# A pooled attention with a gated convolution FFN: pooling and gate sums shared between VectorE and GpSimd in pieces, the late gates by Sigmoid, and a new order of all the work

## The chip, the cores and the metric

The kernel runs on one core of a Trainium2 chip. The metric is the device time in microseconds, the median of several runs of the same kernel. The core has five engines that work from queues of their own, each in order: TensorE (PE in the profile; its weight loads are PEld), VectorE (DVE), ScalarE (ACT), GpSimd (POOL) and SyncE (SP). SyncE, ScalarE and GpSimd also issue DMAs from their queues. Engines wait for each other through semaphores.

## The reference

Eight sequences of 576 positions, eight heads of 64. Keys and values are averaged over eight positions, so attention is over 72 pooled keys; its result feeds an FFN whose hidden layer is gated by the sigmoid of a three-tap convolution along the sequence.

```python
def _attn_ref(q, k, v):
    B, H, S, D = q.shape                      # 8, 8, 576, 64
    k_p = k.reshape(B, H, S // 8, 8, D).mean(axis=3)
    v_p = v.reshape(B, H, S // 8, 8, D).mean(axis=3)
    scores = np.matmul(q, k_p.transpose(0, 1, 3, 2)) / np.sqrt(D)
    scores = scores - np.max(scores, axis=-1, keepdims=True)
    attn = np.exp(scores)
    attn = attn / (np.sum(attn, axis=-1, keepdims=True) + 1e-09)
    return np.matmul(attn, v_p)

def _moe_ref(x, w_in, conv_w, w_out):         # x: 8 x 576 x 512, w_in: 512 x 1024
    h = np.maximum(x @ w_in, 0.0)
    hp = pad(h, one row of zeros at both ends)
    conv_out = sum(conv_w[j] * hp[:, j:j + S] for j in range(3))
    gate = 1.0 / (1.0 + np.exp(-conv_out))
    return h * gate @ w_out
```

## The kernel before

**Order.** The kernel first describes its work as a graph of operations (`Graph.add`): each has the engines that may do it, what it must follow, and the buffers that it uses. A long list, `Graph.ORDER`, then says in which order the operations are emitted and, by the last bit of each number, on which of two engines; `Graph.PLACES` says which buffer of a ring, or which PSUM bank, each one gets, and `Graph.FORMS` which of two matmul shapes. Nothing is planned while the program is built: the lists are the outcome of a planner that ran earlier. Since every engine takes its queue in order, an operation that waits holds back all that stands behind it on its engine.

**Tiles.** The sequences go in four pairs, called groups g = 0 to 3. A group has nine attention tiles of 128 rows (group 0 has ten), 37 in all. Each tile holds all eight heads.

**Preparing.** All inputs are loaded by DMAs that GpSimd issues (`load_q`, `load_v`, `load_pair`, lines 272 to 308), which also convert to bfloat16. For v, VectorE adds halves three times (L471: 1280, 640 and 320 elements a partition) and spreads the sums under a mask of heads (`prep_v`, L475). For k of sequences 2 to 7 it does the same on a pair at once (`pool_pair`, L424: 2304, 1152, 576 elements), and TensorE turns the result (L430, L453); k of sequences 0 and 1 is pooled by a matmul with a pooling matrix. q is turned by TensorE (L501, L505) and copied out of PSUM by VectorE or ScalarE (L519), or by a DMA in group 3.

**Attention, one tile.** Scores on TensorE (L567, L580); the maximum on VectorE (L593); the shift by it on VectorE (L605) or, in group 0, on TensorE (L613); Exp on ScalarE (L631); a transpose by TensorE (L642) and a copy (L656), or by a DMA from SyncE's queue in groups 2 and 3; the product with v on TensorE (L667); a reciprocal and a division on VectorE (L680, L682); and a second transpose to xT, by TensorE (L699) and a copy (L707), or by DMA.

**FFN, one sequence.** For each of eight blocks of 128 hidden channels: eight matmuls of 288 columns (L712) and a ReLU on ScalarE (L721) into hT. The gate is made for four blocks (a half, `f4`) at a time, in one of two ways:
- *by TensorE* (`ffn_conv`, L874): 64x64 matmuls with diagonal weights. Because of the way in which these are packed, the gate of every second block comes out with its two halves of partitions swapped. Tanh (L899) writes even blocks to gT and odd ones to a tile tg; then VectorE adds one to the even ones (L910, 1152 elements) and adds one and swaps for the odd ones (L912, two instructions of 64 partitions). Sequences 4 to 7 have copies at both ends of hT, made on GpSimd (`ffn_wrap`, L796, L797), so that each tap is one run of columns.
- *by taps* (six halves of sequences 4 to 7, `TAPS`): ScalarE multiplies by the middle tap (L847), VectorE adds the two others (L849), Tanh (L854), and VectorE adds one (L860, 2304 elements).

Sigmoid is thus made as (1 + tanh(x/2)) / 2, with the half in the ReLU's scale. VectorE multiplies the gate by h (L920, L861), and TensorE multiplies by w_out for each of 36 row tiles (`ffn_out`, L928, eight matmuls of 512 columns); the result is copied (L939) and stored (L951), mostly from SyncE's queue.

There are two buffers each for hT, gT and xT, one for k, three for v, four for q.

Of the kernel before, what the change touches and what calls it, by code (L numbers as in the profile page):

```python
# [16 lines left out]

# [6 lines left out]
class Op:  # L24
    def __init__(self, engines, key, emit, uses, mode, land, count):
        self.engines, self.key, self.emit, self.mode, self.land, self.count = engines, key, emit, mode, land, count
        self.uses, self.next, self.left = list(uses), [], 0
        self.forms, self.like, self.dmas = None, None, 1
        self.ready, self.start, self.end, self.engine = 0.0, None, None, None
        for t in self.uses:  # L30
            t.users.append(self)


class Graph:

    SPARES = 150
    ATT = 90.28  # L40
    SPREAD = -122.92
    PREP_K = 135.88
    KPOOL = -99.86
    KTURN = 15.09
    PREP_Q = 1123.0
    PREP_V = 2242.18
    GATE = 390.96
    CONV = 199.25
    QCONV = -794.87
    OUT = 412.5  # L50
    LAST = 1107.48
    FIRST = 803.11
    V0 = -1430.11
    DW = -368.65
    X_DMA = 4
    APART = (0,)
    SIXTEEN = ()
    Q_DMA = (3,)
    WRAP = (4, 5, 6, 7)
    TAPS = ((4, 1), (5, 0), (5, 1), (6, 0), (6, 1), (7, 0))  # L60
    ACC = 2
    WRAPS = 2
    CROSS = ()
    BY_TILE = ()
    V_POOL = ()
    K_POOL = ()
    SHIFT_PE = ((0, 0), (0, 1), (0, 2), (0, 3), (0, 4), (0, 5), (0, 6), (0, 7), (0, 8), (0, 9))
    TURN_DMA = 2
    BANKS = 8
    ORDER = (  # L70
# [107 lines left out]
def kernel(  # L178
# [17 lines left out]
    C = 9  # L196
# [1196 lines left out]
```

## Time and profile before

| | |
|---|---|
| median of 3 runs | 220.81 us (220.59 to 220.98) |
| span of the profiled execution, from its first to its last instruction | 224.8 us |
| mean granted TensorE clock in it | 0.979 |
| last copy of a result ends | 220.3 us after the span's start |

The profiled execution has no other time of its own than its span; the span is longer than the timed runs, since the profiler was on. Rows of the profile name the line of the kernel, the engine and operation, the tiles written and read, the count, the busy time and the mean of one; behind the bar stands the engine's idle time just before them and what ended most of it.

### The profile page before, as it was taken

The numbers are of one execution on the slowest core, as the hardware profiler recorded it, in microseconds if no ns is written. First come the engines' busy times: TensorE is split into PE (matmuls) and PEld (weight loads), VectorE is DVE, ScalarE is ACT, GpSimd is POOL, SyncE is SP. The second block draws the span as 40 slices with busy tenths as digits, with TensorE's granted clock in tenths as the row PEclk, the third lists the DMA queues.
The fourth block names the chain that finished last, engine by engine and source line by source line (L and its number), as shares of the span: only waits on it lengthen the run. The fifth ranks groups of instructions, "written<-read, shape, count | busy, mean of one in ns | idle before, by whom it ended". The sixth has DMA issues, their size and how long they took to land.

```text
span 224.8 us, 6558 instructions
## 1 busy us (share of the span) xinstructions
PE 205.1 (91%) x2722; PEld 137.9 (61%) x2722; DVE 195.4 (87%) x337; ACT 160.9 (72%) x271; POOL 45.1 (20%) x81
## 2 busy tenths in 40 slices
PE   5897999979999999959999949989999999999991
PEld 1465778755788877636677735656656665654450
DVE  7889876999999999957999948999999999999641
ACT  2155768898999958844697935688889999997210
POOL 7943321131230120000000121001031230540000
PEclk9999999999999999988999988999999999999997
DMA  5999999999999999947664553168566617423495
GB/s 81 137 191 207 207 206 208 207 207 206 207 208 206 155 187 172 207 39 163 121 106 92 119 118 76 32 92 165 117 145 140 137 23 166 95 48 71 96 247 194
DMA packets 48833, 32.61 MB, mean 145 GB/s; under 512 B 28300, under 2 KB 44324, under 8 KB 48804
## 3 DMA queue, kind: packets, MB, share of 16 engines
q0 software_dynamic: 16288, 16.26, 44.8%
q1 hardware_dynamic: 31796, 14.96, 33.3%
q10 hardware_dynamic: 720, 0.98, 1.5%
q8 instruction: 21, 0.34, 0.6%
q14 instruction: 8, 0.07, 0.1%
HBM read 32.52 MB, written 9.44 MB: 187 GB/s over the span
## 4 chain that ended last, share of the span: by engine, by line
PE 44%; DVE 30%; DMA 8%; issue 7%; ACT 6%; POOL 3%; DVEq 0%; POOLq 0%
PE psum L928 21%; PE psum L712 14%; DVE negm L593 6%; DMA qp<-in_q_dram 6%; DVE x L682 5%; DVE sd L605 5%; PE psum L874 4%; DVE tg L849 2%; DVE gT L912 2%; PE psum L667 2%; DMA eT<-e 2%; DVE v L471 2%; DVE r L680 2%; DVE gT L920 2%; ACT e L631 1%
## 5 line engine op out<-in xcount | busy, mean ns | idle before, releaser
L712 PE MATMUL psum<-xT,w_in_sb 128*128 128x288 bf16 x512 | 74.4, 289 | 0.8 <-ACT tg L899 0.5
L928 PE MATMUL psum<-w_out_sb,gT 128*128 128x512 bf16 (+1 forms) x296 | 70.3, 378 | 0.5 <-DVE gT L920 0.5
L712 PEld LDWEIGHTS <-w_in_sb 128*128 128x128 bf16 x512 | 48.4, 99 | 17.6 <-issue 1.6
L721 ACT ACTIVATE hT<-psum 128x576 bf16<-128x576 f32 x64 | 40.1, 652 | 14.9 <-PE psum L712 14.3
L928 PEld LDWEIGHTS <-gT 128*128 128x128 bf16 x296 | 27.7, 98 | 27.0 <-issue 1.2
L849 DVE SCALAR_TENSOR_TENSOR tg<-hT,convw,tg 128x576 f32<-128x576 bf16 x48 | 37.3, 818 | 0.4
L593 DVE TENSOR_REDUCE negm<-psum 128x8 f32<-128x576 f32 (+2 forms) x37 | 27.4, 750 | 4.4 <-PE psum L567 3.9
L796 POOL COPY hT<-hT 128x126 bf16<-128x126 bf16 x16 | 9.1, 567 | 101.4 <-ACT hT L721 90.9
L682 DVE TENSOR_TENSOR x<-psum,r 128x512 bf16<-128x512 f32 (+1 forms) x37 | 25.6, 691 | 1.3
L667 PE MATMUL psum<-vm,eT 128*128 128x130 bf16 (+5 forms) x240 | 20.0, 227 | 4.1 <-DMA eT<-e 2.9
L874 PE MATMUL psum<-hT,dw 64*64 64x288 bf16 (+2 forms) x608 | 19.2, 261 | 2.6 <-issue 2.3
L667 PEld LDWEIGHTS <-eT 128*128 128x128 bf16 (+1 forms) x240 | 16.0, 103 | 9.1 <-DMA eT<-e 3.8
L605 DVE TENSOR_TENSOR sd<-psum,negm 128x576 f32<-128x576 f32 x27 | 20.1, 752 | 1.0 <-ACT e L631 0.5
L631 ACT ACTIVATE e<-sd 128x576 bf16<-128x576 f32 x27 | 18.6, 689 | 1.8 <-DVE sd L605 1.6
L874 PEld LDWEIGHTS <-dw 64*64 64x64 bf16 x608 | 14.8, 107 | 7.6 <-issue 6.7
L847 ACT ACTIVATE tg<-hT,convw 128x576 f32<-128x576 bf16 x24 | 18.0, 773 | 1.0 <-DVE gT L912 0.9
L899 ACT ACTIVATE tg<-psum 128x576 bf16<-128x576 f32 x20 | 13.0, 653 | 7.2 <-PE psum L874 7.2
L939 ACT COPY osb<-psum 128x512 f32<-128x512 f32 x25 | 14.5, 586 | 4.0 <-PE psum L928 3.9
L854 ACT ACTIVATE gT<-tg 128x576 bf16<-128x576 f32 x24 | 16.2, 685 | 0.8 <-DVE tg L849 0.3
L471 DVE TENSOR_TENSOR v<-v 128x1280 bf16<-128x1280 bf16 (+2 forms) x24 | 13.0, 540 | 2.1 <-DMA v<-in_v_dram 1.9
L899 ACT ACTIVATE gT<-psum 128x576 bf16<-128x576 f32 x20 | 12.9, 649 | 2.0 <-PE psum L874 2.0
L920 DVE TENSOR_TENSOR gT<-gT,hT 128x2304 bf16<-128x2304 bf16 x10 | 13.5, 1349 | 0.0
(82 smaller groups left out, 236.2 us busy)
## 6 DMA issues: line engine op xcount, KB each, us to landing
out_dram<-osb SPq DMA_DIRECT2D x54, 128.0 KB, 2.4
v<-in_v_dram POOLq DMA_DIRECT2D x8, 512.0 KB, 15.2
qp<-in_q_dram POOLq DMA_DIRECT2D x7, 576.0 KB, 16.9
kk<-in_k_dram POOLq DMA_DIRECT2D x3, 1152.0 KB, 17.6
out_dram<-qp SPq DMA_DIRECT2D x10, 128.0 KB, 2.9
w_in_sb<-in_moe_w_in_dram POOLq DMA_DIRECT2D x2, 512.0 KB, 17.3
w_out_sb<-in_moe_w_out_dram POOLq DMA_DIRECT2D x1, 1024.0 KB, 24.3
out_dram<-qp ACTq DMA_DIRECT2D x6, 128.0 KB, 2.7
```

What stands on the lines that cost most here:

```text
L593: nc.vector.tensor_reduce(out=a["m"][0:rows], in_=a["s"][0:rows, :, 0:2 * KW].rearrange("p a (h s) -> p a h s", s=Sp), axis=AX.X, op=OP.ma ...
L605: nc.vector.tensor_tensor(out=a["d"][0:rows], in0=a["s"][0:rows, :, 0:2 * KW].rearrange("p a (h s) -> p a h s", s=Sp), in1=a["m"][0:rows]. ...
L631: nc.scalar.activation(out=dst, in_=src, func=ACT.Exp, scale=1.0 / (POOL * 8.0),)
L667: nc.tensor.matmul(out=a["o"][lo:hi, h // 4, (h % 4) * (D + 1):(h % 4 + x1 - x0) * (D + 1)], lhsT=a["eT"][:, j, lo:hi], rhs=buf("vm", b)[: ...
L682: nc.vector.tensor_tensor(out=a["x"][0:rows].rearrange("p (a h d) -> p a h d", a=2, d=D), in0=ov[:, :, :, 0:D], in1=r[0:rows].unsqueeze(3) ...
L712: nc.tensor.matmul(out=banks(ps)[:, j, 0:SC], lhsT=w_in_block(dc, fb), rhs=buf("xT", g)[:, dc, i * S + j * SC:i * S + (j + 1) * SC], start ...
L721: nc.scalar.activation(out=h_of(b)[:, fb].rearrange("p (a s) -> p a s", a=2), in_=banks(ps)[:, :, 0:SC], func=ACT.Relu, scale=0.5,)
L847: nc.scalar.activation(out=acc, in_=h, func=ACT.Identity, scale=w)
L849: nc.vector.scalar_tensor_tensor(out=acc, in0=h, scalar=w, in1=acc, op0=OP.mult, op1=OP.add)
L874: nc.tensor.matmul(out=banks(pss[r ^ c])[c * D:(c + 1) * D, j, lo:hi], lhsT=dw[r * D:(r + 1) * D, tap * n_fb + fb, :], rhs=hT[r * D:(r + 1 ...
L899: nc.scalar.activation(out=t.rearrange("p (a s) -> p a s", a=2), in_=banks(ps)[:, :, 0:SC], func=ACT.Tanh, scale=0.5,)
L928: nc.tensor.matmul(out=bank(ps)[0:rows, columns], lhsT=buf("gT", g)[:, fb, t * P:t * P + rows], rhs=w_out_sb[:, fb, columns], start=(fb == 0),
```

## The change

1. **Pieces on two engines.** The three additions of k and v and the spread of v are cut (k: three, two and one pieces; v: two, one, one and two), and each piece may be done by VectorE or GpSimd, as the order says. The three raisings of a gate (adding one, and the swap) become operations of their own that may go to either engine too.
2. **Sigmoid for late gates.** For sequences 5, 6 and 7 ScalarE computes Sigmoid instead of Tanh. The adding of one falls away there; only the swap of odd blocks stays, as a copy. ReLU has the scale 1 there instead of 0.5. Sigmoid and Exp are in different function tables, so all Sigmoids follow all Exps, and one table load stands between them.
3. **Choices by tile.** Shift, both transposes and the form of the gate are chosen tile by tile in a table, `CHOICE`. ReLU may go to VectorE, clearing to GpSimd, stores of all groups to ScalarE's queue.
4. **No end copies for the gates made by TensorE**; 64 matmuls for a pair of blocks everywhere, where sequences 4 and 7 had 48.
5. **A new order**: new lists, made by a planner in which VectorE gives way to GpSimd, and which was run under three sets of durations. The matmuls that filled TensorE's early waits (L384, 22) are no longer in the list.

How many instructions each engine gets, in the two programs:

| | before | after |
|---|---|---|
| VectorE: raisings of gates | 36 | 11 |
| VectorE: pooling and spread of k and v | 41 | 37 |
| GpSimd: raisings of gates | 0 | 20 |
| GpSimd: pooling and spread of k and v | 0 | 29 |
| GpSimd: end copies | 32 | 24 |
| VectorE, ScalarE: copies of turned Exps | 2, 17 | 9, 10 |
| VectorE, ScalarE: ReLU | 0, 64 | 6, 58 |
| ScalarE: table loads | 1 | 2 |
| ScalarE's queue: stores | 9 | 26 |
| TensorE: fills | 22 | 0 |

```diff
-    def pool_pair(g, step):
-        t, half = buf("kk", g), POOL * D >> step + 1
-        engine = nc.gpsimd if g in Graph.K_POOL else nc.vector
+    def pool_pair(g, step, cs, engine):
+        t, half = buf("kk", g)[:, cs], POOL * D >> step + 1
         engine.tensor_tensor(out=t[:, :, 0:half], in0=t[:, :, 0:half], in1=t[:, :, half:2 * half], op=OP.add)
...
+    def raise_gate(engine, b, fb, out, in_):
+        if graph.chosen("sigma", b, fb // 4):
+            engine.tensor_copy(out=out, in_=in_)
+        elif engine is nc.gpsimd:
+            engine.tensor_scalar(out=out, in0=in_, scalar1=1.0, scalar2=1.0, op0=OP.mult, op1=OP.add)
+        else:
+            engine.tensor_scalar(out=out, in0=in_, scalar1=1.0, scalar2=None, op0=OP.add)
...
+    def gate_func(b, fb):
+        return ACT.Sigmoid if graph.chosen("sigma", b, fb // 4) else ACT.Tanh
...
-    def ffn_gate(b, f4):
+    def ffn_gate(b, f4, part, engine):
...
-        nc.vector.tensor_scalar(out=gate[:, 0], in0=gate[:, 0], scalar1=1.0, scalar2=None, op0=OP.add)
-        for r in range(2):
-            nc.vector.tensor_scalar(
-                out=gate[r * D:(r + 1) * D, 1], in0=tg[(1 - r) * D:(2 - r) * D], scalar1=1.0, scalar2=None, op0=OP.add
-            )
+        if part == 2:
+            raise_gate(engine, b, 4 * f4, gate[:, 0], gate[:, 0])
+            return
+        raise_gate(engine, b, 4 * f4, gate[part * D:(part + 1) * D, 1], tg[(1 - part) * D:(2 - part) * D])
...
+    def fast(instructions, n, two=True):
+        return {"DVE": instructions * (0.065 + n * (0.00052 if two else 0.00026)),
+                "POOL": instructions * (0.1 + n * (0.00198 if two else 0.00091))}
...
+        for step, cuts in ((0, (0, 3, 6, 9)), (1, (0, 5, 9)), (2, (0, 9))):
+                o = add(fast(1, (hi - lo) * (POOL * D >> step + 1)), None, after=before or [loads["kk", g]], uses=[kk[g]])
+                then(o, lambda o, step=step, cs=cs: pool_pair(g, step, cs, hand(o)))
...
+        for step, cuts in enumerate(((0, 3, 5), (0, 5), (0, 5), (0, 3, 5))):
+                o = add(fast(1, (hi - lo) * (POOL * D >> step + 1 if step < 3 else 3 * D)), None,
...
+    for o in sigmas:
+        for e in exps:
+            graph.follow(e, o)
```

Here `fast` holds the durations that the planner worked with for the divisible operations, `hand` gives the engine that the order chose, and `sigmas` and `exps` are all Sigmoid and all Exp operations.

More of the change, by code (lines that the diff above doesn't have):

```diff
@@ L24, with __init__ @@
 class Op:
-    def __init__(self, engines, key, emit, uses, mode, land, count):
-        self.engines, self.key, self.emit, self.mode, self.land, self.count = engines, key, emit, mode, land, count
+    def __init__(self, engines, emit, uses, mode, land, count):
+        self.engines, self.emit, self.mode, self.land, self.count = engines, emit, mode, land, count
         self.uses, self.next, self.left = list(uses), [], 0
-        self.forms, self.like, self.dmas = None, None, 1
-        self.ready, self.start, self.end, self.engine = 0.0, None, None, None
+        self.forms, self.dmas, self.engine = None, 1, None
         for t in self.uses:
@@ L985, with add_load @@
-    seq = [START]
-    def nudge(kind, b):
-        return 0.0
-    def soon():
-        seq[0] += 0.01
-        return seq[0]
-    loads = {}
-    kk, kp, qp, qTt = {}, {}, {}, {}
-    kb = B and H * S * D * 4
-    def add_load(kind, b, key, share=1.0, **part):
+    n_outs = {b: [t for t in range(9) if (t < 4) == (i == 0)] for b, (g, i) in where.items()}
+    kb = H * S * D * 4
+    loads, kp, qp, qTt = {}, {}, {}, {}
+    kk0 = token("kk", 0)
+    kk = {0: kk0}
+    def add_load(kind, b, share=1.0, **part):
@@ L1032 @@
-    p0 = add({"POOL": 1.6}, first("pm"), build_pool_matrix, after=[c1])
-    add_load("q", 0, first("q0"), 4 / 9, cs=slice(0, 4))
-    c0 = add({"POOL": 0.55}, first("ident"), lambda: make_identity(nc, ident))
-    z0 = add({"DVE": 0.3}, soon(), lambda: clear(buffers["kT"][0]))
-    idf = add({"ACT": 0.3}, soon(), lambda: nc.scalar.copy(out=ident_f, in_=ident), after=[c0])
-    cwtok = token("ps")
-    cwp = add({"PE": 0.1}, soon(), lambda: turn_conv_weights(cwtok), after=[idf, cwl], uses=[cwtok], count=2)
@@ L1047 @@
-    hmw = add(dve(1.15), soon(), widen_mask, after=[hm])
-    dw0 = add({"DVE": 0.3}, soon(), lambda: build_conv_matrices(0, cwtok), after=[cwp], uses=[cwtok])
-    dwo = [add({"DVE": 1.0}, START + Graph.DW + n, lambda n=n: build_conv_matrices(n), after=[dw0]) for n in (1, 2)]
-    win = [add({"POOL": 0.74}, first("w%d" % j), lambda j=j: load_w_in(j), land=(LATE, 2 * P * d_ff * 4, RATE)) for j in range(2)]
-    wout = add({"POOL": 0.9}, first("out"), load_w_out, land=(LATE, d_ff * d_model * 4, RATE))
@@ L1053, in add_load_pair @@
+    def add_load_pair(g):
         kk[g] = token("kk", g)
[L1054 to L1057 removed]
+        loads["kk", g] = add({"POOL": 1.03}, lambda: load_pair(g), uses=[kk[g]], land=(1.3, 2 * kb, 1))
+    for b in range(1, B):
         if b == 1:
[L1059 to L1063 removed]
@@ L1211, in add_att @@
-        xdone[g, t] = o
-    hdone, gdone, htok, gtok = {}, {}, {}, {}
+        for by_dma in graph.options("out", (0, 1) if g else (0,), g, t):
+            if by_dma:
+                outs.append(add({"SP": 1.29}, lambda: att_out(g, t), after=[o], uses=[x, xtok[g]], land=(1.4, 0, 1)))
+            else:
+                sm2 = token("ps")
+                p = add({"PE": 0.223}, lambda sm2=sm2: att_turn_out(g, t, sm2), after=[o], uses=[sm2, x],
+                        mode=FULL if rows == P else (64, 128), count=8)
+                p = add(either(0.42, 0.59), None, after=[p], uses=[sm2, xtok[g]])
+                outs.append(then(p, lambda p: att_copy_out(g, t, copier(p))))
@@ L1308, in add_out @@
-    def add_out(b, w):
-        w += nudge("o", b)
+        relu = {}
+        for fb in range(n_fb):
+            big, o = token("ps", n=2), None
+            for j in range(2):
+                o = add({"PE": 0.49}, lambda fb=fb, j=j, big=big: ffn_in(b, fb, j, big),
+                        after=half_of(b, j) + [win[fb // 4], o], uses=[big, xtok[g]], mode=FULL, count=8)
+            o = add({"ACT": 0.565, "DVE": 0.665}, None, after=[o], uses=[big, htok[b]])
+            relu[fb] = [then(o, lambda o, fb=fb, big=big: ffn_relu(b, fb, big, o))]
@@ L1344 @@
[L1344 to L1359 removed]
+            o = add(either(0.69, 0.585), None, after=[o] + free, uses=[osb, sm])
@@ new lines, in add_out, with queue @@
+            then(o, lambda o, t=t, sm=sm: ffn_copy(g, t, sm, copier(o)))
+            o = add({"SP": 1.3, "ACT": 1.16}, None, after=[o], uses=[osb], land=(2.4, 0, 1))
+            then(o, lambda o, t=t: ffn_store(g, t, queue(o)))
+    def queue(o):
+        return nc.scalar if o.engine == "ACT" else nc.sync
+    for b in range(B):
+        if b < 2:
+            add_prep_k(b)
+        elif b % 2 == 0:
+            add_pair(b // 2)
+        add_prep_q(b)
+        add_prep_v(b)
+    for b in range(B):
+        for t in n_tiles[b]:
+            add_att(where[b][0], t)
@@ L1361 @@
+    for b in range(B):
+        add_ffn(b)
+        add_out(b)
+    for o in sigmas:
+        for e in exps:
+            graph.follow(e, o)
     with tc.manual_schedule():
```

687 lines of the change are left out of this document (294 added, 393 removed), and 121 rows, old and new, of tables (ORDER, PLACES).

## Prediction

> **What bounds the kernel now.** I read the page's span and busy rows first, then the windows, then the end of the chain of waits. The windows' columns are the stretch, its length, and each engine's busy time with its instruction count; then the granted clock, the DMA share and GB/s.
>
> ```profile
> span 224.8 us, 6558 instructions
> PE 205.1 (91%) x2722; PEld 137.9 (61%) x2722; DVE 195.4 (87%) x337; ACT 160.9 (72%) x271; POOL 45.1 (20%) x81
> PE 44%; DVE 30%; DMA 8%; issue 7%; ACT 6%; POOL 3%; DVEq 0%; POOLq 0%
> 0.00:40.00 40.00, 33.98 (x572) 24.07 (x575) 32.35 (x78) 21.61 (x36) 19.20 (x37) 1.00 1.11 177
> 40.00:166.60 126.60, 118.05 (x1799) 83.02 (x1788) 115.72 (x196) 98.81 (x168) 15.45 (x28) 0.97 0.84 145
> 0.00:166.60 166.60, 152.03 (x2359) 107.08 (x2360) 148.06 (x273) 120.42 (x203) 34.66 (x65) 0.98 0.91 153
> 163.10:219.90 56.80, 56.60 (x384) 32.45 (x380) 50.42 (x70) 43.55 (x74) 12.24 (x20) 1.00 0.51 120
> 162.82 0.30 PE L567 MATMUL psum<-kT,qT 64*64 64x72 bf16 x16
> 180.01 1.47 PE psum L712 x12
> 179.15 0.86 PE psum L928 x4
> 219.85 0.42 DVE qp L939
> ```
>
> The kernel has two long stages. From 163.1 us, when the last attention tile's scores leave TensorE (the L567 row), to 219.9 us, TensorE is busy 56.6 of 56.8 us, and at its peak: the chain gives 1.47 us for 12 matmuls of L712 (0.1225 each) and 0.86 for 4 of L928 (0.216 each). After those scores the built program has 128 of L712, 180 of L928, 24 of L667 and 48 of L874; 128 x 0.1225 + 180 x 0.216 is 54.6 us, which leaves 2.2 for the other 72, about 0.03 each. This stage is as long as TensorE's work in it.
>
> Ahead of that, from 40 to 166.6 us (the last maximum), VectorE is busy 115.7 of 126.6 us. TensorE's 118.1 is no better evidence: a small matmul shows its latency as busy time (that stage has 1799 in 118 us, the last one 384 in 57), and the chain of waits gives VectorE 30% of the span, most of it in this stage. So the time of the last scores is VectorE's, and the rest of the span is TensorE's. The span is 4.0 us above the median of the timed runs, 220.81; I sum against the span and multiply by 220.81 / 224.8 = 0.982.
>
> **The change on VectorE.** I counted both built programs' VectorE instructions ahead of the last maximum, and priced them by these rows (pieces of other sizes by a line through the three sizes of L471 and L424: some 0.15 us + 0.52 ns an element).
>
> ```profile
> L849 DVE SCALAR_TENSOR_TENSOR tg<-hT,convw,tg 128x576 f32<-128x576 bf16 x48 | 37.3, 818 | 0.4
> L920 DVE TENSOR_TENSOR gT<-gT,hT 128x2304 bf16<-128x2304 bf16 x10 | 13.5, 1349 | 0.0
> L912 DVE TENSOR_SCALAR gT<-tg 64x1152 bf16<-64x1152 bf16 x20 | 9.1, 455 | 0.3
> L910 DVE TENSOR_SCALAR gT<-gT 128x1152 bf16<-128x1152 bf16 x10 | 5.3, 530 | 0.0
> L860 DVE TENSOR_SCALAR gT<-gT 128x2304 bf16<-128x2304 bf16 x6 | 4.8, 800 | 0.1
> L471 DVE TENSOR_TENSOR v<-v 128x1280 bf16<-128x1280 bf16 x8 | 6.5, 818 | 1.9 <-DMA v<-in_v_dram 1.9
> L471 DVE TENSOR_TENSOR v<-v 128x640 bf16<-128x640 bf16 x8 | 3.9, 485 | 0.1
> L471 DVE TENSOR_TENSOR v<-v 128x320 bf16<-128x320 bf16 x8 | 2.5, 318 | 0.1
> L475 DVE TENSOR_TENSOR vm<-v,mask_wide 128x960 bf16<-128x960 bf16 x8 | 5.2, 651 | 0.1
> L424 DVE TENSOR_TENSOR kk<-kk 128x2304 bf16<-128x2304 bf16 x3 | 4.0, 1347 | 0.0
> L682 DVE TENSOR_TENSOR x<-psum,r 128x512 bf16<-128x512 f32 x35 | 24.2, 692 | 1.2
> L519 DVE COPY qT<-psum 128x1152 bf16<-128x1152 bf16 x4 | 3.0, 751 | 0.7 <-PE psum L501 0.7
> L656 DVE COPY eT<-psum 128x640 bf16<-128x640 bf16 x1 | 0.5, 480 | 0.0
> L939 DVE COPY osb<-psum 128x512 f32<-128x512 f32 x2 | 1.4, 683 | 0.0
> ```
>
> - Gate sums (L912 18 to 5, L910 9 to 2, L860 1 to none): 13 x 0.455 + 7 x 0.530 + 0.8 = 10.4 us off.
> - Pooling of v and its spread (L471 and L475, 18.2 us in 32 instructions) becomes 25 smaller ones, 11.0 us: 7.2 off. Pooling of k (7.7 us in nine) becomes twelve, 6.2: 1.5 off. The clearing of e goes to GpSimd: 0.5 off.
> - Copies that come to VectorE: seven of eT (3.5 us, less one short one), three of qT (2.0), two of osb (1.4), one ReLU (about 0.7); two of kT leave (0.6): 7.0 us on.
> - Order: 7 fewer of L849, 2 fewer products L920, 2 fewer divisions and one shift stand ahead of the last maximum: 5.7 + 2.7 + 1.8 + 0.7 = 11 us later, not saved.
>
> That is 23.6 us less. By the same rows the program before sums to 160.6 us there, while the windows give 148.06 busy: neighbours overlap, so a summed microsecond is 0.92 elapsed, and 23.6 become 21.7. Over the whole program the counts fall by 12.9 us summed, 11.9 elapsed; the rest is order.
>
> **On TensorE.** The later work comes back behind the last scores: the changed program has 168 of L712 there, 200 of L928, 36 of L667 and 96 of L874. That is 40 x 0.1225 + 20 x 0.216 + 60 x 0.03 = 11.0 us more, 67.8 in all. Ahead of them it loses these 11.0 and the fills' 7.8 (row below) from its 152.0 busy: 133, which fits into the 145 to 150 us that VectorE will need. Behind them VectorE holds about 57 us and ScalarE about 50, DMA issues included; both stay under 67.8, so I put nothing there for the Sigmoid's table load (1.28 us, below), the six ReLUs on VectorE or nine stores moved to ScalarE's queue at 1.2 us a pair. If that cover went, these would cost about 1.3, 4 and 11 us.
>
> ```profile
> L1036 ACT ACT_TABLE_LOAD x1 | 1.3, 1283 | 0.8 <-PEq L1377 0.8
> 212.23 1.21 ACTq L951 DMA_DIRECT2D out_dram<-qp  x2
> L384 PE MATMUL psum<-gT 128*128 128x448 bf16 x22 | 7.8, 463 | 2.8 <-DVE gT L1027 2.5 <-ACT eT L656 0.2
> ```
>
> Sigmoid takes as many ScalarE instructions as Tanh, and saves the raising of five four-block groups (L860, 0.8 each): inside the VectorE counts. Two half-sequences give up their wrapping copies on GpSimd (8 of 32), and their convolution takes 64 matmuls a pair of blocks instead of 48, counted in L874. All Sigmoids wait for the last Exp; 17 ReLUs remain behind it against 15 before, so the wait moves no bound. The 22 filling matmuls (L384, 7.8 us) go; they stood where TensorE waited for loads. Without them the first real matmuls may run slower, and the second half of k now queues on GpSimd behind the pooling matrix: I put 0.6 us for both, from 0 to 2.
>
> **What GpSimd costs VectorE.** GpSimd gets 20 raisings of 1152 elements and 29 additions and products of 15,744 elements in all. Rows that show what two such engines do to each other (min/median/max in ns):
>
> ```profile
> 4.20 1.66 POOL L316 TENSOR_SCALAR_AFFINE_SELECT gT<-gT 64x648 bf16<-64x648 bf16 x2
> 4.28 0.78 DVE L372 TENSOR_TENSOR ident<-ident 128x64 bf16<-128x64 bf16 x1
> L376 DVE TENSOR_TENSOR dw<-ident,convw x2: 948/1257/1566, 5.1 to 30.1; 128x768 bf16<-128x768 bf16 x2
> L910 DVE TENSOR_SCALAR gT<-gT x10: 441/452/911, 42.5 to 207.8; 128x1152 bf16<-128x1152 bf16 x10
> L796 POOL COPY hT<-hT x16: 294/530/1452, 126.9 to 201.7; 128x126 bf16<-128x126 bf16 x16
> L849 DVE SCALAR_TENSOR_TENSOR tg<-hT,convw,tg x48: 800/814/892, 130.4 to 204.2; 128x576 f32<-128x576 bf16 x48
> ```
>
> VectorE's addition of 64 elements at 4.28 us took 0.78, until GpSimd's first selection was over; its next one took 1.57 against 0.95 without a neighbour. GpSimd's 0.29 us copies took up to 1.45 beside VectorE. So the one that starts second waits. The Trainium skill says it as a rule, in "SBUF — State Buffer", section "Who interferes with whom": VectorE instructions with two SBUF inputs, or in a mode with two ports, and GpSimd instructions that read SBUF lock each other out for a whole instruction, and those that read PSUM never wait. By that rule the trace agrees.
>
> In the stage from 40 us to the last maximum 48 of the changed VectorE instructions are of that kind (12 of k, 10 of v, 3 spreads, 7 raisings, 8 products, 8 taps); some 118 read PSUM, among them the maxima and divisions. Unit price from below: beside the late copies L849 never lost more than 0.892 - 0.800 = 0.09 us; 48 x 0.1 = 4.8. From above: the three hits above cost 0.5 to 0.7 us. GpSimd's own rate is not shown for these forms; L316 gives 1.2 ns an element with one input, so 28 us for the raisings and 19 to 38 for the two-input pieces, 47 to 66 us, about half of a stage of 100: half of 48 at 0.6 is 14.4. I take 4.8, because the copies too run beside a busy VectorE, in an order, not at random; below zero nothing can come of it.
>
> The Trainium skill's "GPSIMD Engine Reference", section "Performance versus the Vector engine", gives about 2.6 cycles an element for two inputs at 1.2 GHz: an estimate of 34 us for the 15,744 elements. That lies inside the bounds above and moves no term.
>
> **Sum.** 224.8 - 21.7 + 11.0 + 4.8 + 0.6 = 219.5 us of span, times 0.982: 215.6 us.
>
> **Rivals.**
> 1. *The lock costs more than was saved* (slower). Break-even is where lock and start cost 10.7 us, or 0.21 us for each of the 48. For it: a piece of 1 us or more is longer than the 0.29 us copies. At 14.4 the time is 225.0; at 20 it is 230.5. Against it: 118 neighbours that read PSUM, beside which a piece can run. Chance 0.18. The Trainium skill's rule, applied to an order that does not avoid it, is this case.
> 2. *GpSimd's queue becomes late* (slower). It executes in order, and each wait for ScalarE's gates, a landed load or the port holds every load and piece behind it.
>
> ```profile
> POOL v L290 <- DVE vm L475: 13.9, 2, 7.2
> v<-in_v_dram POOLq DMA_DIRECT2D x8, 512.0 KB, 15.2
> ```
>
>    A v load takes 15.2 us to land, and such loads already waited 13.9 us for free buffers. With 47 to 66 us of pieces and some 25 of issues, GpSimd has 72 to 91 of about 100 us. If one chain of k or v comes one load late, TensorE loses up to 15 us: 230; one half late, 223. Chance 0.10.
> 3. *A gain beyond the forecast*: the order hides the lock and the start entirely, 224.8 - 21.7 + 11.0 = 214.1, which is 210.3; and if a third of VectorE's 10.9 us of idle between 40 and 166.6 us goes too, 206.7. Chance 0.15.
> 4. *Nothing left over*: order and lock cancel the relief; 220 to 221.5. Chance 0.10, of which 0.04 within the bound, 0.04 faster, 0.02 slower.
>
> The forecast, a lock of 2 to 8 us, gives 212.8 to 218.7; chance 0.47. Between these, the sum says 0.66 for faster by over 0.2% (0.2%, 0.44 us, is about what a measurement of this kernel can tell), 0.04 for no difference, 0.30 for slower. The range that leaves out no more than 2 in 10 goes from 209.5 to 226.
>
> **What would show it.** Right: VectorE's busy time about 182 (195.4 - 11.9 and some waiting), the last scores (line L552 of the changed kernel) near 147 us, then a TensorE stage of 68 us without gaps, raisings on GpSimd of 1 to 1.5 us. Wrong: products and taps on VectorE well above 1.36 and 0.82 us (rival 1); idle VectorE or TensorE that GpSimd's pieces end (rival 2); gaps behind the last scores that a Sigmoid ends.

## The result and the profile after

The changed kernel takes 230.64 us (median of 4 runs, 229.07 to 231.72) against 220.89 for the kernel before, measured beside it: ratio 1.0448, 95% interval 1.0388 to 1.0507. It is 4.5% slower. The forecast was 215.6 us, with a range that ended at 226. The medians here and below are over all runs, while the ratios leave out runs that lie over 1.5% above the fastest of the same kernel.

The page of the changed kernel: span, busy rows, and the chain that ended last, by engine.

```profile
span 228.8 us, 6686 instructions
PE 200.4 (88%) x2752; PEld 139.5 (61%) x2768; DVE 192.7 (84%) x318; ACT 150.7 (66%) x253; POOL 105.0 (46%) x128
PE 54%; DVE 20%; issue 8%; DMA 8%; ACT 4%; POOL 3%; ACTq 0%; DVEq 0%; POOLq 0%
```

VectorE was forecast at some 182 us busy and has 192.7. This execution took 230.63 us, its span plus 1.83, and the three others took 1.82 to 1.87 us more than their spans. So the note ahead of the prediction, that the span is longer than the runs because the profiler was on, is wrong: a span of 224.8 us belongs to a run of some 226.6 us, and the profiled execution of before was a long one. Another execution of the unchanged kernel before (e1_before, 222.17 us) is the better partner. These are its window up to the last maximum, the line of the scores, whose last start is 158.5 us, and in the timeline the last copy of a result.

```profile
0.00:162.10 162.10, 149.30 (x2342) 106.85 (x2359) 147.43 (x273) 120.13 (x203) 35.47 (x65) 1.00 0.93 157
```

```profile
L567 PE MATMUL psum<-kT,qT x312: 189/195/217, 12.5 to 158.5; 64*64 64x72 bf16 x156
```

```profile
215.43 0.42 DVE L939 COPY qp<-psum 128x256 f32<-128x256 f32 x1 [0.46 <-PE psum L928]
```

The changed kernel has these rows for the same, with the window behind the last scores:

```profile
0.00:157.30 157.30, 134.83 (x2272) 100.60 (x2281) 134.54 (x239) 100.60 (x172) 90.52 (x106) 0.96 0.95 155
155.90:224.10 68.20, 66.98 (x504) 40.01 (x500) 59.15 (x81) 51.25 (x84) 14.83 (x23) 1.00 0.53 118
```

```profile
L552 PE MATMUL psum<-kT,qT x296: 190/195/265, 14.4 to 155.8; 64*64 64x72 bf16 x148
```

```profile
224.12 0.42 DVE L891 COPY qp<-psum 128x256 f32<-128x256 f32 x1 [0.96 <-PE psum L880]
```

Behind the last scores TensorE is busy 66.98 of 68.20 us; 67.8 was forecast. Before, that stage lasted from 158.5 to about 215.4, 57 us. Ahead of them the change was to save 16.3 us (21.7 less 4.8 and 0.6) and saved 2.7 (158.5 to 155.8). The whole miss lies there. VectorE's busy time up to the last maximum did fall by 12.9 us (147.43 to 134.54), but its idle time rose by 8.1 (14.7 to 22.8). By the forecast 21.7 - 4.8 = 16.9 us were to come off, and all of it was to shorten the front.

The groups that answer the questions on GpSimd (line, engine, operation, count, busy time, mean in ns):

```profile
L785 POOL TENSOR_SCALAR gT<-tg 64x1152 bf16<-64x1152 bf16 x11 | 15.1, 1375 | 4.7 <-ACT tg L853 4.0
L872 DVE TENSOR_TENSOR gT<-gT,hT 128x2304 bf16<-128x2304 bf16 x16 | 26.4, 1656 | 0.0
L410 DVE TENSOR_TENSOR kk<-kk 128x768 bf16<-128x768 bf16 x6 | 4.8, 824 | 0.0
L410 DVE TENSOR_TENSOR kk<-kk 128x640 bf16<-128x640 bf16 x3 | 2.4, 802 | 0.0
L410 DVE TENSOR_TENSOR kk<-kk 128x512 bf16<-128x512 bf16 x1 | 1.4, 1402 | 0.0
L787 DVE TENSOR_SCALAR gT<-tg 64x1152 bf16<-64x1152 bf16 x7 | 4.0, 574 | 0.2
L815 DVE SCALAR_TENSOR_TENSOR tg<-hT,convw,tg 128x576 f32<-128x576 bf16 x48 | 37.6, 815 | 0.6
```

The products take 1.656 us in the mean against 1.349 before: 16 x 0.307 is 4.9 us. The mean hides two kinds: five of them take 2.26 to 2.44 us, the other eleven 1.35 to 1.36. VectorE's additions of v, which nothing disturbed, take 0.550, 0.484 and 0.417 us for 768, 640 and 512 elements in this trace; by these those of k lost 1.6, 1.0 and 1.0, and the gate sums 7 x 0.119 = 0.8. That is 9.3 us of locked VectorE time. All but one product's 0.95 us of it, some 8.4 us, stands ahead of the last maximum, where 4.8 was taken and 14.4 was the upper bound. The taps (L815) lost nothing.

Three stretches show where TensorE stands. First the kernel before (e1_before), then the changed one:

```profile
40.00:60.00 20.00, 17.32 (x323) 12.04 (x316) 19.08 (x32) 18.30 (x32) 4.07 (x5) 1.00 1.24 207
70.00:80.00 10.00, 9.73 (x173) 8.17 (x172) 9.74 (x21) 8.90 (x17) 1.01 (x1) 1.00 1.00 159
130.00:140.00 10.00, 9.46 (x94) 5.97 (x96) 8.96 (x16) 6.23 (x11) 1.92 (x5) 1.00 0.48 100
```

```profile
40.00:60.00 20.00, 15.82 (x402) 12.61 (x395) 15.64 (x27) 13.82 (x24) 12.68 (x16) 0.83 1.09 183
70.00:80.00 10.00, 7.71 (x133) 6.00 (x132) 8.70 (x13) 6.03 (x12) 9.67 (x8) 0.83 1.07 133
130.00:140.00 10.00, 8.20 (x117) 5.86 (x115) 9.41 (x13) 6.42 (x12) 5.57 (x6) 0.90 0.50 81
```

In these 40 us TensorE of the changed kernel is busy 4.8 us less, and what it does it does at a granted clock of 0.83, 0.83 and 0.90 where before had 1.00. Each holds one pause of 1.8 to 2.3 us and half clock in it or behind it.

### The profile page after: what moved, and what is told of

Its sections match the earlier page's. It is cut to its first block, busy times and chain, and to the rows that moved or that the text cites. A ratio compares the mean times of both kernels' runs of the same rounds, so it can differ in the third digit from the quotient of the medians.

```text
span 228.8 us, 6686 instructions
## 1 busy us (share of the span) xinstructions
PE 200.4 (88%) x2752; PEld 139.5 (61%) x2768; DVE 192.7 (84%) x318; ACT 150.7 (66%) x253; POOL 105.0 (46%) x128
## 4 chain that ended last, share of the span: by engine, by line
PE 54%; DVE 20%; issue 8%; DMA 8%; ACT 4%; POOL 3%; ACTq 0%; DVEq 0%; POOLq 0%
PE psum L880 21%; PE psum L697 18%; DVE x L667 5%; PE psum L838 4%; DMA out_dram<-osb 4%; DMA v<-in_v_dram 4%; PE psum L652 3%; DVE kk L410 2%; DVE gT L872 2%; DVE negm L578 2%; DVE sd L590 2%; PE psum L684 2%; PE psum L627 2%; DVE r L665 1%; DVE gT L787 1%
## 5 line engine op out<-in xcount | busy, mean ns | idle before, releaser
L880 PE MATMUL psum<-w_out_sb,gT 128*128 128x512 bf16 (+1 forms) x280 | 65.9, 373 | 1.2 <-issue 0.5
L713 ACT ACTIVATE hT<-psum 128x576 bf16<-128x576 f32 x58 | 37.3, 650 | 12.6 <-PE psum L697 12.2
L815 DVE SCALAR_TENSOR_TENSOR tg<-hT,convw,tg 128x576 f32<-128x576 bf16 x48 | 37.6, 815 | 0.6
L578 DVE TENSOR_REDUCE negm<-psum 128x8 f32<-128x576 f32 (+3 forms) x37 | 27.4, 754 | 9.5 <-PE psum L565 4.5
L872 DVE TENSOR_TENSOR gT<-gT,hT 128x2304 bf16<-128x2304 bf16 x16 | 26.4, 1656 | 0.0
L590 DVE TENSOR_TENSOR sd<-psum,negm 128x576 f32<-128x576 f32 (+1 forms) x26 | 19.6, 755 | 1.8 <-ACT e L616 0.5
L616 ACT ACTIVATE e<-sd 128x576 bf16<-128x576 f32 (+1 forms) x26 | 17.6, 681 | 4.1 <-DVE sd L590 1.5
L785 POOL TENSOR_SCALAR gT<-gT 128x1152 bf16<-128x1152 bf16 x9 | 11.5, 1280 | 18.9 <-ACT gT L820 15.7
L456 POOL TENSOR_TENSOR v<-v 128x320 bf16<-128x320 bf16 (+3 forms) x14 | 18.2, 1304 | 2.1 <-DVE v L456 1.5
L820 ACT ACTIVATE gT<-tg 128x576 bf16<-128x576 f32 x24 | 16.3, 682 | 3.3 <-DVE tg L815 3.3
L891 ACT COPY osb<-psum 128x512 f32<-128x512 f32 x20 | 11.6, 580 | 8.8 <-PE psum L880 7.3
L785 POOL TENSOR_SCALAR gT<-tg 64x1152 bf16<-64x1152 bf16 x11 | 15.1, 1375 | 4.7 <-ACT tg L853 4.0
## 6 DMA issues: line engine op xcount, KB each, us to landing
qp<-in_q_dram POOLq DMA_DIRECT2D x7, 576.0 KB, 14.7
kk<-in_k_dram POOLq DMA_DIRECT2D x3, 1152.0 KB, 16.3
```

The costliest lines, as they stand in the source:

```text
L456: engine.tensor_tensor(out=vt[:, :, 0:half], in0=vt[:, :, 0:half], in1=vt[:, :, half:2 * half], op=OP.add)
L578: nc.vector.tensor_reduce(out=a["m"][0:rows], in_=a["s"][0:rows, :, 0:2 * KW].rearrange("p a (h s) -> p a h s", s=Sp), axis=AX.X, op=OP.ma ...
L590: nc.vector.tensor_tensor(out=a["d"][0:rows], in0=a["s"][0:rows, :, 0:2 * KW].rearrange("p a (h s) -> p a h s", s=Sp), in1=a["m"][0:rows]. ...
L713: nc.scalar.activation(out=out, in_=banks(ps)[:, :, 0:SC], func=ACT.Relu, scale=scale)
L785: engine.tensor_scalar(out=out, in0=in_, scalar1=1.0, scalar2=1.0, op0=OP.mult, op1=OP.add)
L815: nc.vector.scalar_tensor_tensor(out=acc, in0=h, scalar=w, in1=acc, op0=OP.mult, op1=OP.add)
```

## The experiments

All times are medians; the ratio is to the kernel before, measured beside each.

**The bases: e1_before and e10_after**, both kernels unchanged.

> The kernel before, unchanged, profiled once more. Theory A (the profiled execution of before was a long one): the span is about 219.0, since the changed kernel's runs take 1.83 us more than their span, and 220.8 less 1.83 is 219.0; the stalls near 96 us and 129 us are then shorter. Theory B (before's profiled execution was a typical one and its span stands 4 us above its runs): the span is 224 to 225 again, with both stalls. Time 220.8 in both.

> The changed kernel, unchanged, once more, as the base of these runs: 229 to 233, with TensorE's pause of about 2.3 us in the middle of the transposes L490 near 50 us, and the half clock behind it, if that pause belongs to the program; without it, if it was chance.

e1_before: 221.84 us, ratio 0.9964 (0.9907 to 1.0021), with a span of 220.4. Theory A holds in kind: the profiled execution of before was 4.4 us longer than this one. e10_after: 230.71, ratio 1.043 (1.033 to 1.053), and the pause near 50 us is there again, 2.37 us at the same transposes. It belongs to the program.

**Is VectorE the bound of the front? e11_before_relief, e15_before_conv1, e20_both.** The kernel before, with work left out on VectorE, on TensorE, and on both.

```diff
 # e11: no pooling additions (pool_pair, prep_v steps 0 to 2)
+        return
 # e15: conv_todo, both forms
-for tap in (1, 0, 2)
+for tap in (1,)
 # e20: both edits
```

> The kernel before, with VectorE's 33 additions that pool k and v left out (20.6 us of VectorE, all ahead of the last maximum; GpSimd, ScalarE and the order as before; k and v are not pooled). If VectorE alone sets the time of the last maximum, as the prediction had it, 221 less 0.92 x 20.6 = 19: 201 to 205. If round trips between the engines stand right behind it, the relief is paid only in part: 207 to 217, VectorE's idle time ahead of the last maximum rising from 14.7 us to 20 or more.

> The kernel before with only the middle tap of the convolution in its matmul form (the outer taps are left out there): some 420 small TensorE matmuls less, most of them ahead of the last scores, VectorE and the rest as before. Theory D (TensorE is the bound of the front): 0.0215 us each, 8 to 10 us off, 211 to 214. The prediction's view (VectorE sets the time of the last scores): 219 to 221, since only what lies behind the last scores counts.

> The kernel before without VectorE's 33 pooling additions and without the outer taps of the matmul form of the convolution (k and v are not pooled, the convolution is not complete). If VectorE and TensorE stand level in the front, the two reliefs pay together what neither paid alone: 207 to 213. If loads or round trips hold both: 216 to 219, no more than the 3 us of the taps alone.

Measured: 220.93 (ratio 1.0018, 0.9969 to 1.0067); 218.36 (0.9883, 0.9845 to 0.992); 214.87 (0.9695, 0.9619 to 0.9771). Taking 20.6 us of work from VectorE ahead of the last maximum moved nothing. This is the run that refutes the prediction's first step. Its window up to the last maximum stands first, then the chains by engine of e1_before, e11, e15 and e20, each over the whole span:

```profile
0.00:161.00 161.00, 150.23 (x2361) 106.98 (x2362) 131.42 (x240) 120.02 (x203) 35.47 (x65) 1.00 0.95 158
```

```profile
PE 38%; DVE 36%; DMA 10%; issue 8%; ACT 5%; POOL 0%; DVEq 0%
```

```profile
PE 52%; DVE 21%; DMA 8%; issue 6%; ACT 6%; POOL 3%; SPq 0%; DVEq 0%; POOLq 0%
```

```profile
DVE 51%; PE 22%; issue 12%; DMA 5%; ACT 5%; POOL 3%; DVEq 0%; ACTq 0%; POOLq 0%
```

```profile
DVE 34%; PE 27%; DMA 16%; ACT 9%; issue 8%; POOL 4%; DVEq 0%; ACTq 0%; POOLq 0%
```

With VectorE relieved its busy time falls to 131.4 of 161 us, and the chain goes from VectorE (36 to 21%) to TensorE (38 to 52%); with TensorE relieved, it goes to VectorE (51%). Neither relief alone pays more than 3 us (0 and 2.6 by the ratios); together they pay 6.4 (6.7 by the ratio), more than the sum of both and still short of the 8 us at the near end of what was expected, and then the chain holds 16% of landing loads. So the front of before has VectorE and TensorE level within a few us, with the loads and round trips not far behind. What I expected of e15 (8 to 10 us) was too much for the same reason.

**What the pieces on GpSimd bring in the new order: e2_all_dve, e3_gate_dve, e14_k_dve.** The changed kernel, its pieces back on VectorE: all, the gate sums, the pooling of k.

```diff
             o.engine = list(o.engines)[0 if n < 0 else n % 2]
+            if o.kind in Graph.BACK:     # ("k", "v", "gate"), ("gate",), ("k",)
+                o.engine = "DVE"
```

> The changed kernel in its own order, with every divided piece that GpSimd does (29 of the pooling of k and v and its spread, 20 gate sums, the clearings) on VectorE, some 22 us more work there by VectorE's own rows. Theory A (what GpSimd takes off VectorE comes back nearly whole, as locked VectorE instructions, some 10 us, and as waits for late pieces): 227 to 234, products L872 back at 1.35 us. Theory B (the pieces do save VectorE's time, and the new order and the start lose it again): 240 to 250. Theory C (late pieces of GpSimd are most of the loss): under 224.

> The changed kernel in its own order, with only the 20 gate sums of GpSimd back on VectorE (20 x 0.46 to 0.53, 10 us more there). Theory A: the sums beside the products make much of the lock, so 226 to 233, and L872 near 1.4 us. Theory B: 236 to 241. Theory C: under 225 if the late pieces are gate sums, about 240 if they are k and v.

> The changed kernel with only GpSimd's pieces of k's pooling back on VectorE (some 5 to 6 us more there). Theory D, if the pause at 75 us (2.19 us, ended by a k addition) comes from late or locked pieces: it falls under 1 us, and the time is 227 to 230 in spite of the added work. If VectorE is the bound there: 233 to 237.

Measured: 243.89 (ratio 1.0992, 1.0899 to 1.1085), 233.96 (1.0561, 1.0464 to 1.0659) and 234.83 (1.0628, 1.0543 to 1.0714). In the order that was made for them the pieces are worth 13 us in all; theories A and C fall for e2, and B was right. e3 came out between A and B. So GpSimd as such is not where the time goes: the kernel is slower in spite of it. e14's time is that of its last case, VectorE as the bound: the pause at 75 us did fall, from 2.19 to 1.27 us, but others of about 2 us came at 79 and 126.

**The pieces left out: e5_left_out, e18_half_left.** GpSimd's in-place additions of k and v and its nine in-place gate sums return without an instruction; e18 has the transposes of e13 (below) as well.

```diff
 # pool_pair, prep_v (steps 0 to 2), ffn_gate part 2, raise_gate on one view
+        if engine is nc.gpsimd:
+            return
```

> The changed kernel in its own order; GpSimd's in-place pieces (its additions of k and v, and 9 gate sums gT<-gT) are left out, so part of the pooling and of the gate sums is not computed; 11 gate sums out of tg and the spreads stay. VectorE's own instructions are the same. Theory A: the lock and the waits for those pieces go, 8 to 13 us, 217 to 223, the pooling additions on VectorE back at 0.56 for 768 elements. Theory B: 228 to 231, no more than 2 us less. Theory C: 217 to 222 with locked instructions as long as before, the gain being idle time of VectorE and TensorE.

> As e13_half_q, with GpSimd's in-place pieces left out (its k and v additions and 9 gate sums are not computed; 11 gate sums and the spreads stay). The lock and the late pieces together: 221 to 224. If the order is what is left: 225 to 227.

Measured: 231.71 (ratio 1.0298, 1.0157 to 1.0438) and 228.75 (1.0244, 1.0156 to 1.0332). The products of e18, and a TensorE row of it:

```profile
L880 DVE TENSOR_TENSOR gT<-gT,hT 128x2304 bf16<-128x2304 bf16 x16 | 21.6, 1356 | 0.0
```

```profile
101.96 0.45 PE L656 MATMUL psum<-vm,eT 128*128 128x130 bf16 x2 [3.60 <-DMA eT<-e]
```

The lock went for the most part (products at 1.356, in e5 1.350; additions of 640 elements at 0.487, but those of 768 still at 0.710, where 0.55 was expected), but the time did not follow: TensorE now waits 3.60 us for a transposing transfer of eT (5.10 in e5). Work that leaves one place of a fixed order made another late. The traces are of executions of 229.84 us (e18) and 235.21 us (e5), both above their medians. These two runs are inconclusive on the price of the lock, and why that transfer comes late stays open.

**GpSimd in an order not made for it: e8_before_gate_gp.** The kernel before, `ffn_gate` on GpSimd.

```diff
-        nc.vector.tensor_scalar(..., scalar1=1.0, scalar2=None, op0=OP.add)
+        nc.gpsimd.tensor_scalar(..., scalar1=1.0, scalar2=1.0, op0=OP.mult, op1=OP.add)
```

> The kernel before, in its own order, with the 30 gate sums of the matmul form on GpSimd (14.4 us off VectorE, some 36 us of GpSimd). Theory D: no gain, since TensorE is the bound, and some loss where locked products and late sums hold TensorE: 221 to 227, L920 at 1.5 us or more against 1.35. The prediction's view: 0.92 x 14.4 = 13 off less a lock of up to 8: 209 to 217.

Measured: 226.59, ratio 1.026 (1.0213 to 1.0307). The time is as theory D had it, the reason is not: the products run at 1.352 us, unlocked, and five of the ten wait for their sums. The row of the products, and the wait:

```profile
L920 DVE TENSOR_TENSOR gT<-gT,hT x10: 1346/1352/1359, 45.4 to 209.8; 128x2304 bf16<-128x2304 bf16 x10
DVE gT L920 <- POOL gT L912: 9.8, 5, 3.5
```

**The pause near 50 us: e13_half_q, e19_half_again, e12_fills.** It stands in the middle of the transposes L490, with no wait on it ("issue"). In the list of forms nine of the ten q transposes of sequences 1 to 5 use the smaller form, 36 matmuls with 36 weight loads (72 instructions); in the kernel before it was four of the ten, the others in 18 larger matmuls (36 instructions). TensorE's timeline of the changed kernel around it (start, length, line, tile, count, idle time before it), and the row of the instruction queue:

```profile
44.50 0.28 PE L838 MATMUL psum<-hT,dw 64*64 64x224 bf16 x2 [0.58 <-issue]
44.51 0.90 PE L490 MATMUL psum<-ident,qp 64*64 64x64 bf16 x72
45.49 0.47 PE L416 MATMUL psum<-pick,kk 128*64 128x64 bf16 x18
46.14 0.52 PE L652 MATMUL psum<-vm,eT 128*128 128x130 bf16 x6 [0.18 <-DVE qT L504]
46.50 0.38 PE L684 MATMUL psum<-ident,x 128*128 128x128 bf16 x4
47.16 0.19 PE L552 MATMUL psum<-kT,qT 64*64 64x72 bf16 x1 [0.28 <-DVE kT L429]
47.59 0.32 PE L552 MATMUL psum<-kT,qT 64*64 64x72 bf16 x15 [0.23 <-ACT kT L429]
48.01 0.28 PE L490 MATMUL psum<-ident,qp 64*64 64x64 bf16 x10
50.55 0.58 PE L490 MATMUL psum<-ident,qp 64*64 64x64 bf16 x26 [2.26 <-issue]
```

```profile
q8 instruction: 21, 0.34, 0.6%
```

From the first "issue" to the second there are 2 + 72 + 18 + 6 + 4 + 16 + 10 = 128 matmuls, with their weight loads 256 instructions. The instruction queue moved 21 packets of 0.34 / 21 = 0.016 MB; TensorE's 5520 instructions (2752 + 2768) are 21.6 times 256. Other runs fit: e12 has 5568 and moved 22 packets, e13 5212 and 20, e15 4548 and 18. So a packet is one block of 256 instructions, and TensorE pauses where its next block has not landed. The trace shows it: its four gaps without a wait between 28 and 57 us stand ahead of the 351st, 607th, 735th and 863rd matmul, whole multiples of 128 apart, and at each a block's packet had ended only 1.29 to 1.43 us before TensorE went on (1.35 to 1.40 in e10_after). Here one block lasts 3.8 us (44.50 to 48.29) while the DMA engines are full (share 1.23 in the mean from 40 to 57 us), and the next packet starts only 3.6 us after the block's first matmul; at the 863rd and the 1503rd, with a share of 0.7, it starts after 1.3 and 0.5 us. That loads hold the packets back fits this, but no run varied the loads.

```diff
-                    o.forms = [(HALF, 0.53, 36), (QUARTER, 0.32, 72)]
+                    o.forms = [(HALF, 0.53, 36), (HALF, 0.53, 36)]     # e13, e19
 # e12: order(), behind the clearing of the fills' operand
+                for s in self.early: ...     # 16 fills, bank 7
```

> The changed kernel with the q transposes of sequences 1 to 5 all in the 36-matmul form, where some use 72 smaller ones. Theory D (TensorE is the bound from 30 us on, and the change loses its time in three pauses near 50, 75 and 138 us; the one near 50 comes because many small instructions meet a full DMA): the pause in L490 shrinks below 1 us or goes, with the half clock behind it, 226 to 229. Theory E (the pause is not tied to the number of instructions): it stays, and the longer transposes make it 230 to 232.

> e13_half_q once more, the base of these runs: 225 to 227, with both pauses.

> The changed kernel with 16 filling matmuls at the start, as before had them; nothing else moves. If the start without fills costs what it was put at, 0.6 us: 229 to 231. If it costs 2 or more: 227 to 229. The pause in the middle of L490 near 50 us: if it hangs on the place in TensorE's instruction stream, it comes 32 instructions (16 matmuls and their loads) earlier; if it hangs on data, at the same transposes.

Measured: e13 225.79, ratio 1.0215 (1.0148 to 1.0282); e19, the same kernel, 224.6, 1.0143 (1.0054 to 1.0232); e12 232.63, 1.0514 (1.0431 to 1.0596). e13 from 40 to 60 us, and the pause of e12:

```profile
40.00:60.00 20.00, 18.57 (x424) 15.34 (x415) 18.89 (x34) 17.30 (x30) 14.81 (x19) 1.00 1.08 181
```

```profile
50.05 0.33 PE L556 MATMUL psum<-kT,qT 64*64 64x72 bf16 x6 [1.59 <-issue]
```

With the fills the pause comes with 6 scores and 10 transposes still to do that stood ahead of it before: 16 matmuls earlier, exactly the fills that were put in. It hangs on the place in the instruction stream. With the larger form it is gone, the clock is 1.00, and the time is 4.9 us (e13) to 6.1 us (e19, a little under the 225 to 227 expected) shorter, half of the loss or more. The traces show how much of that falls at the pause. VectorE's maximum that starts at 47.96 us in the changed kernel starts at 48.24 in e13 and 46.94 in e19; the one at 59.49 starts at 56.03 and 54.73. So the changed kernel loses 3.7 us against both within these 12 us; the rest comes and goes with the execution (the start, the half clock below). It is not less work: the q transposes keep TensorE busy for 9.2 us in e13 and 5.1 + 2.6 in the changed kernel. The fills themselves bring nothing.

**The other two pauses: e16_apart.** In the changed kernel, first the pause at 75.5 us, with what VectorE and GpSimd did ahead of it; then the one at 137.9:

```profile
70.47 2.31 DVE L872 TENSOR_TENSOR gT<-gT,hT 128x2304 bf16<-128x2304 bf16 x1
71.66 3.48 POOL L785 TENSOR_SCALAR gT<-tg 64x1152 bf16<-64x1152 bf16 x2
72.71 1.43 DVE L410 TENSOR_TENSOR kk<-kk 128x640 bf16<-128x640 bf16 x1
75.50 0.47 PE L416 MATMUL psum<-pick,kk 128*64 128x64 bf16 x18 [2.19 <-DVE kk L410]
```

```profile
132.64 2.33 DVE L872 TENSOR_TENSOR gT<-gT,hT 128x2304 bf16<-128x2304 bf16 x1
132.61 1.15 POOL L785 TENSOR_SCALAR gT<-gT 128x1152 bf16<-128x1152 bf16 x1 [0.20 <-ACT gT L853]
135.00 1.29 DVE L787 TENSOR_SCALAR gT<-tg 64x1152 bf16<-64x1152 bf16 x1
133.85 2.13 POOL L785 TENSOR_SCALAR gT<-tg 64x1152 bf16<-64x1152 bf16 x1
137.87 1.53 PE L697 MATMUL psum<-xT,w_in_sb 128*128 128x288 bf16 x6 [1.80 <-DVE sd L590]
```

In the first, the product lost 0.96 us and the k addition behind it 0.94, together 1.90 of the pause's 2.19. In the second, the product lost 0.98 and the gate sum 0.83, 1.81 against a pause of 1.80. e16 has the transposes of e13, and just these four sums of GpSimd on VectorE, late in its queue.

```diff
-ORDER: ..., 1059 (sum, POOL), ..., 1179 (POOL), ..., 1325 (POOL), ..., 1329 (POOL), ..., 1330 (product)
+ORDER: ..., 1058 (DVE), 1178 (DVE), ..., 1324 (DVE), 1328 (DVE), 1330
```

> As e13_half_q, with four of GpSimd's 20 gate sums on VectorE: the two that ran at 68.2 us, beside a product and a k addition (2.31 and 1.43 us there), and the two at 130.4 and 131.7 us, beside a product and a gate sum (2.34 and 1.29 us); the last two stand behind the shift that TensorE waits for. If the lock makes the pauses at 72 and 136 us: the product and the additions are back at 1.35 and 0.49 us, both pauses fall below 1 us, and the time is 222.5 to 224.5. If the pauses come from the order: they stay, 225 to 227.

Measured: 224.45, ratio 1.0056 (1.0000 to 1.0112), some 1.2 us above before. Two rows of it, VectorE's addition and TensorE's first pause:

```profile
67.91 0.48 DVE L401 TENSOR_TENSOR kk<-kk 128x640 bf16<-128x640 bf16 x1
```

```profile
69.65 0.47 PE L407 MATMUL psum<-pick,kk 128*64 128x64 bf16 x18 [1.12 <-DVE kk L401]
```

The addition is back at 0.48, the pause at 70 us fell from 2.19 to 1.12 (the product there stayed at 2.31, beside another piece, so that it did not fall below 1 us as expected), and the one near 136 us is gone. So half of the first pause and all of the second go with these locked sums. What that is worth in time is not clear of noise. By the ratios it is 0.9 to 1.6% (against e19 and e13), 2 to 3.5 us, but the intervals of e16 and e19 overlap; e16's ten runs go from 220.61 to 230.38 us, its median is 0.15 us below e19's, and its profiled execution is 1.4 us shorter than e19's (222.31 and 223.74).

**The same form in the kernel before: e17_before_half_q**, the edit of e13 there.

> The kernel before with the q transposes all in the 36-matmul form. If the gain in e13 is the instruction stream's (pauses at every 128th matmul while the DMA engines are full), the pause at 98 us moves or shrinks: 219 to 221.5. If the longer form is itself the cheaper one: 2 us or more off, 217 to 219.

Measured: 220.34, ratio 0.9991 (0.9956 to 1.0027): no difference that the ratio can tell. But the kernel before has such a pause too (2.29 us at 98.3 us in its first profile, 1.84 in e1_before):

```profile
98.41 0.53 PE L874 MATMUL psum<-hT,dw 64*64 64x288 bf16 x13 [1.84 <-issue]
```

In e17 no TensorE gap above 1.0 us is left behind the start, and its ten runs lie between 219.57 and 221.15, where the 19 runs of before beside them go from 218.71 to 226.23. So the larger form alone is no gain of 5 us; what it brings in the changed kernel, it brings by the pause.

**Stores by SyncE: e6_store_sp.**

```diff
+            if o.kind == "store":     # groups 0 to 2
+                o.engine = "SP"
```

> The changed kernel with all output stores of groups 0 to 2 issued by SyncE, none by ScalarE. If stores that ScalarE issues late hold the output buffers, and so VectorE (the wait of 1.82 us at 106.6 us, and 9.5 us of the chain on landing stores): 225 to 229. If SyncE's queue then delays the transposes behind the stores, 232 to 236. Nothing: 229 to 232.

Measured: 232.72, ratio 1.0528 (1.0455 to 1.06). Issued by SyncE alone the stores are no better: the wait of 1.8 us for an output buffer stayed (1.9). So nothing points to the stores on ScalarE's queue as a cause of the loss.

No version beat the kernel before by more than its interval; e17 and e16 come nearest.

## Why the prediction was wrong, point by point

- **What bounds the front: the step that failed.** I read 115.7 busy of 126.6 us on VectorE as its bound, put TensorE's 118.1 aside as latency, and let every microsecond off VectorE shorten the front. e11_before_relief took off 20.6 and got nothing; e20_both shows two engines level, and more behind. The chain could not tell: from 40 to 163 us it gave VectorE some 60 us and TensorE 33 (more than half of TensorE's 44% is the last stage), but a chain shows one path, and a second one of nearly its length does not appear in it. The sign was in the busy row that I put aside: two engines, each busy over 90% of a stage, can both be its bound, and here they were.
- **TensorE ahead of the last scores.** "133, which fits into the 145 to 150 us" was right as a count (134.8) and wrong as a fit. In e1_before TensorE does 149.3 less 7.9 of fills, 141.4 us of work, and has 20.7 us without any; after, 134.8 and 22.5. Moving work behind the last scores made that stage longer at once (68.2 us, as forecast) and the front hardly shorter.
- **VectorE's relief and the lock.** The counts held: 195.4 - 11.9 + 9.3 of lock is 192.8, and the page has 192.7. The lock term was mis-sized: 8.4 us ahead of the last maximum (9.3 in all) for 4.8, inside its bounds. Where a locked product or addition stood right ahead of something TensorE waited for, it made a pause; the four sums that e16 takes away were worth 3.5 us at the most. So rival 1 named a real mechanism, with a break-even that rested on the failed step.
- **What was not priced at all: the form of the q transposes.** The list of forms stood in the change, and a pause of 2.29 us with nothing to wait for stood in the trace of before (98.3 us). I priced neither; the larger form gives back 4.9 to 6.1 of the 9.8 us, 3.7 of them at the pause itself.
- **Rival 2** (GpSimd's queue late) did not happen in this order: no product of the changed kernel waited for a sum. It did in e8, with 9.8 us of waits.
- **The start and the fills**: 0.6 us was put down; giving 16 fills back gained nothing (e12). **The table load of Sigmoid** was covered, as said: no gap behind the last scores is ended by a Sigmoid.
- **The factor 0.982** was wrong. The time is the span plus 1.6 to 1.9 us in nearly every run, and the profiled execution was a long one. With e1_before as the base the same sum gives 220.4 - 21.7 + 11.0 + 4.8 + 0.6 + 1.8 = 216.9, so this is not what put the forecast on the wrong side.

Added up: the larger form takes the changed kernel from 230.7 to 225.8 or 224.6 us, and without the four sums it is at 224.45, 1.2 us above before by the ratio and 2.8 by the medians. That rest stays open. All of this only brings it back to the kernel before; that nothing is gained beyond it is the failed step, a VectorE relief that by itself shortens nothing.

## What to carry to other kernels

Before a stage is called bound by one engine, leave that engine's work out in a run, or at least see whether a second engine is as busy: with two level engines a relief of one was worth 0 and 2.6 us here. Count instructions as well as work: here TensorE stalled where it used up a block of 256 instructions in 3.8 us while loads filled the DMA engines. The lock between VectorE and GpSimd made TensorE pause where the locked instruction stood right ahead of something that TensorE waited for, so look for those few pieces first.

## What the runs showed of the hardware that was not expected

- **Instruction blocks.** TensorE paused 2.26 us between two blocks of 128 matmuls with their loads (2.37 in e10_after), and 16 added matmuls moved the pause by 16 matmuls. The Trainium skill, "Runtime: NRT & Kernel Launch", section "Instruction fetch mechanics", gives blocks of 256 instructions, fetched by DMA ahead of use, at a cost that is mostly hidden. The count agrees with the trace; hidden it was not: at each gap the block's packet had ended only some 1.4 us before.
- **The clock around a short pause.** In the pause of 2.26 us the granted clock fell to 0.50, at 49.2 us, and stayed there until 56 us; one row of that time stands below. The Trainium skill, "TensorE: Matmul & The Clock Gate", section "Part 1: The HAM clock gate", speaks of an idle window of about 3.4 us; here less was enough, for TensorE was busy for 1.68 of the 3.41 us ahead of the fall. Whether half clock follows a pause differs between executions of one program, and where it did, time was lost: behind the third pause the changed kernel had a clock of 0.58 from 138 to 142 us, e10_after 1.00 from 140 to 144, and between the product at 139.41 us (141.52 in e10_after) and the maximum at 155.91 (155.65) the changed kernel lost 2.4 us against it. The mean clock of a run does not show that: runs at 0.966 and 0.993 took 230.63 and 230.66 us.

```profile
51.00:52.00 1.00, 1.00 (x19) 0.94 (x10) 0.24 (x1) 0.83 (x1) 0.92 (x2) 0.50 1.24 209
```

- **GpSimd loses in the lock too.** Its gate sums take 1.15 us undisturbed. The one at 133.85 us took 2.13, begun while VectorE's product ran until 134.97; VectorE's next sum, begun at 135.00 beside it, took 1.29, where 0.455 is its time alone.
